# Attention states carried by one scan per head pair, in a kernel of attention and two feed-forward layers

## The chip, the core and the metric

The kernel runs on one core of a Trainium2 chip. The metric is device time in microseconds (us), the median of several executions. One more execution was profiled, and all rows of the trace below come from that one. Engines are named as the profile names them: PE (TensorE, matrix products), DVE (VectorE), ACT (ScalarE), POOL (GpSimd) and SP (SyncE, which issues the DMAs).

## What is computed

Three layers follow each other. The first is a gated linear attention with 4 batches, 8 heads, 768 steps and heads of 48; its output is x with 3072 rows of 384.

```python
def _attn_ref(q, k, v, alpha) -> np.ndarray:
    ...
    for t in range(S):
        state = alpha[:, :, t, :, None] * state + np.einsum('bhd,bhe->bhde', k[:, :, t], v[:, :, t])
        y[:, :, t] = np.einsum('bhd,bhde->bhe', q[:, :, t], state)
```

The second layer is `h = x @ w_in; g = h * np.cos(h); x = g @ w_out` with an inner width of 2048. The third is `h = max(x @ w1, x @ w2, x @ w3); h @ w_out` with an inner width of 768. All data are 32 bits wide.

## The kernel before

**Tiling.** The 3072 tokens form 6 blocks (`u`) of 512. Inside a block the attention runs in 8 chunks of 64 steps and in 4 head pairs (`p`; `k` is the order in which they are taken, the last pair first). A batch has 12 chunks, so a state begins anew at chunk 0 of block 0, chunk 4 of block 1, and so on. The two heads of a pair stand at partitions 0 to 47 and 64 to 111.

**One head pair, `att`.** DVE scans alpha into the products `g` (L370 or L380; in block 0 in two halves) and, from their reciprocals, into a second product written over `al` (L376 or L385). POOL multiplies k by `g` (L372 or L384) and q by `al` (L387). PE transposes k (L392, "T" below), ACT brings that from PSUM as `kt` (L395), and PE makes the scores (L404) and the sums of k times v of each chunk (L409) in two PSUM banks `r[0]` and `r[1]` ("K"); chunk c has its sum in bank c mod 2. The scores are masked into `a`: by DVE straight from PSUM (L420), or in blocks `u < MKP` by ACT (L416) and POOL (L417). The states then go from chunk to chunk: `state(c)` is one DVE instruction on 112 by 48 elements (L428, or the copy L426 where a batch begins), eight per head pair and each dependent on the one before. `d` is each chunk's state times that chunk's whole product, by POOL in two instructions (L440; in block 0 one half comes from ACT, L435). PE multiplies `a` with v (L453) and `d` with q (L459) into one result ("V"), which ACT and DVE (in block 0 ACT and PE, L477) split into a high and a low part.

**The feed-forward layers.** Every product of 128 by 128 by 512 is made of three matmuls on high and low parts. Layer two has 16 units per block, `moe1(i)`: 9 matmuls from x (L501 to L503), a cosine on ACT and DVE (L508 to L513 or L517), a high part on ACT (L514 or L518) and a low part on POOL (L515, for units `GLE1 <= i < GLP1`) or on DVE (L523), then 9 matmuls into `acc` (L528 to L530). A weight block is put together from two words by three DVE instructions (L315 to L317), split by ACT (L320) and POOL (L321); the 32 blocks of layer two are made ready during block 0. Layer three follows (L579 to L581, L587 to L591, L602 to L607).

**Order.** Nothing is reordered by hand. `Program` collects operations with an engine, an estimated duration, the names that they read and write, and a due time; `order` walks through them once and gives each engine its queue, which it then runs strictly in order. The due time of an attention step is `ATT0 + ATTS * k` in units of layer two. Two operations that only read the same name are free of each other in that walk.

Of the kernel before, what the change touches and what calls it, by code (L numbers as in the profile page):

```python
# [49 lines left out]
NQ, NG, NRAW, NIN, NV, NGS = 3, 2, 3, 3, 2, 3  # L50
# [10 lines left out]
GLP1 = 20  # L61
# [182 lines left out]
def tile_kernel(ctx, tc, qka, vv, wt, outT):  # L244
# [32 lines left out]
    inv0 = [ap.tile([PR, LINE], F32, name=f"inv{i}")[:, 0:AL].rearrange("p (c t) -> p c t", c=NC) for i in range(2)]  # L277
# [7 lines left out]
    s_b = [ap.tile([PR, NC, D], F32, name=f"s{p}") for p in range(NP)]  # L285
# [56 lines left out]
    def att(u, k, p, t0):  # L342
        m = u * NP + k
        n, n2 = m % NIN, m % 2
        t, kq_, v, kt, a, s, d, iv = al_b[n], kq_b[n], v_b[m % NV], kt_b[n2], a_b[n2], s_b[p], d_b[n2], inv0[n2]
# [77 lines left out]
        def state(c):  # L423
            o, kvc = s[:, (c + 1) % NC], r[c % 2][0:PR, c // 2 * D:(c // 2 + 1) * D]
            if firsts[c]:
                ve.tensor_copy(o, kvc)  # L426
            else:
                ve.scalar_tensor_tensor(o, s[:, c], g[:, c, 0:1], kvc, ALU.mult, ALU.add)  # L428

        for c in range(NC - 1):  # L430
            op("DVE", 0.2, lambda c=c: state(c), [rk[c % 2], *kgs, (*sk, c)], [(*sk, c + 1)], t0 + 0.25)
            if u < DAC and not firsts[c + 1]:
                for j in range(DAH):
                    w = slice(UP * j, UP * j + D)
                    op("Act", act(D) + 0.21, lambda c=c, j=j, w=w: se.activation(d[w, j, c + 1], s[w, c + 1], AF.Copy, scale=g[w, c + 1, 0:1]),  # L435
                       [*kgs, (*sk, c + 1)], [(dk, j, c + 1)], t0 + 0.25)
        for j in range(2):
            if u >= DAC or j >= DAH:
                w = slice(UP * j, UP * j + D)
                op("Pool", pool(NC * D), lambda j=j, w=w: ge.tensor_tensor(d[w, j], s[w], g[w, :, 0:1].to_broadcast([D, NC, D]), ALU.mult),  # L440
                   [*kgs, *[(*sk, c) for c in range(NC)]], [(dk, j, c) for c in range(NC)], t0 + 0.25)
            elif not firsts[0]:
                w = slice(UP * j, UP * j + D)
                op("Act", act(D) + 0.21, lambda j=j, w=w: se.activation(d[w, j, 0], s[w, 0], AF.Copy, scale=g[w, 0, 0:1]), [*kgs, (*sk, 0)], [(dk, j, 0)], t0 + 0.25)
# [166 lines left out]
    def build():  # L611
# [20 lines left out]
        def setup_rest():  # L632
# [132 lines left out]
```

## Time and profile before

| | |
|---|---|
| median of 3 runs | 818.61 us (815.3 to 819.21) |
| profiled execution | 816.9 us, of which the span in the trace is 815.2 us |
| busy in the span | PE 791.5 us (97%), DVE 476.4 (58%), ACT 360.9 (44%), POOL 192.8 (24%) |
| chain that ended last | PE 84%, DVE 6%, POOL 4%, issue 2%, DMA 2%, ACT 2% |

Busy is the time in which an engine runs at least one instruction; a matmul's end is modelled, so a busy PE may still run below its peak. The time outside the span, 1.7 us, is start and end of the execution. [...]

### The profile page before, as it was taken

The page shows a single profiled execution, that of the slowest core. Times are in us where ns is not written, and L with a number is a line of the kernel's source. Part 1 is how long each engine was busy: PE and PEld are TensorE (multiplying, and loading weights), DVE is VectorE, ACT ScalarE, POOL GpSimd, SP SyncE. Part 2 cuts the span into 40 slices and gives each one's busy share as a digit, 9 for nine tenths or more (in the row PEclk, how much of TensorE's full clock was granted, in tenths as well). Part 3 has the DMA queues.
Part 4 walks back from the last instruction along what each step waited for, and adds up shares of the span by engine and source line. Part 5 has one row for each costly group of instructions (what it writes and reads, how often), then busy time and mean ns, then how long its engine had stood idle before and what let it go on. Part 6 is the DMA issues. An engine that isn't in the chain of part 4 may idle for free.

```text
span 815.2 us, 15114 instructions
## 1 busy us (share of the span) xinstructions
PE 791.5 (97%) x6168; PEld 646.0 (79%) x6168; DVE 476.4 (58%) x924; ACT 360.9 (44%) x667; POOL 192.8 (24%) x191
## 2 busy tenths in 40 slices
PE   7679999999999999999999999999999999999998
PEld 6567778888878878888888788888888888888886
DVE  7988999765786587667679955452232222322221
ACT  4575655555645565555577746531121121112121
POOL 7777876530231023101123200110000000000000
PEclk8789999999999999999999999999999999999999
DMA  9745564430242033103135600412020020200001
GB/s 273 214 132 174 182 209 141 130 93 5 88 147 54 2 115 108 43 1 108 34 107 161 221 23 1 156 58 86 26 83 27 14 91 26 78 27 13 14 27 39
DMA packets 26661, 71.86 MB, mean 88 GB/s; under 512 B 3488, under 2 KB 3488, under 8 KB 26592
## 3 DMA queue, kind: packets, MB, share of 16 engines
q1 hardware_dynamic: 26592, 70.90, 26.9%
q8 instruction: 48, 0.79, 0.4%
q14 instruction: 21, 0.17, 0.1%
HBM read 54.37 MB, written 14.16 MB: 84 GB/s over the span
## 4 chain that ended last, share of the span: by engine, by line
PE 84%; DVE 6%; POOL 4%; issue 2%; DMA 2%; ACT 2%; SPq 0%; POOLq 0%; DVEq 0%; ACTq 0%
PE ps L580 9%; PE ps L579 9%; PE ps L581 9%; PE acc L528 7%; PE ps L501 7%; PE acc L530 7%; PE acc L529 7%; PE ps L503 7%; PE ps L502 7%; PE ps L603 3%; PE ps L602 3%; PE ps L604 3%; PE ps L459 2%; PE ps L404 1%; PE ps L453 1%
## 5 line engine op out<-in xcount | busy, mean ns | idle before, releaser
L501 PE MATMUL ps<-xt,wih 128*128 128x512 f32 x288 | 116.3, 404 | 3.7 <-ACT kt L395 2.2
L528 PE MATMUL acc<-gh,woh 128*128 128x512 f32 x288 | 116.5, 405 | 0.7 <-DVE yy L538 0.5
L530 PE MATMUL acc<-gl,woh 128*128 128x512 f32 x288 | 112.8, 392 | 0.5 <-DVE gl L523 0.4
L502 PE MATMUL ps<-xt,wih 128*128 128x512 f32 x288 | 113.2, 393 | 0.0
L503 PE MATMUL ps<-xt,wil 128*128 128x512 f32 x288 | 113.0, 392 | 0.0
L529 PE MATMUL acc<-gh,wol 128*128 128x512 f32 x288 | 112.4, 390 | 0.0
L517 DVE SCALAR_TENSOR_TENSOR ps<-q,ps 128x512 f32<-128x512 f32 x76 | 52.7, 694 | 56.9 <-ACT q L511 56.7
L589 DVE TENSOR_TENSOR ps<-t,ps 128x512 f32<-128x512 f32 x36 | 25.0, 696 | 103.6 <-PE ps L581 103.5
L510 ACT ACTIVATE q<-q 128x512 f32<-128x512 f32 x96 | 60.5, 631 | 52.3 <-DVE q L509 52.0
L508 ACT ACTIVATE q<-ps 128x512 int32<-128x512 f32 x96 | 57.1, 595 | 57.0 <-PE ps L503 54.6
L509 DVE SCALAR_TENSOR_TENSOR q<-q,ps 128x512 f32<-128x512 int32 x96 | 65.7, 685 | 21.1 <-ACT q L508 20.8
L590 ACT ACTIVATE h<-ps 128x512 fp32r<-128x512 f32 x36 | 21.5, 598 | 112.1 <-DVE ps L589 112.0
L523 DVE TENSOR_TENSOR gl<-ps,gh 128x512 fp32r<-128x512 f32 x76 | 52.1, 686 | 26.7 <-PE ps L503 15.9
L501 PEld LDWEIGHTS ps<-xt,wih 128*128 128x128 f32 x288 | 54.7, 190 | 16.4 <-ACT kt L395 3.2
L440 POOL TENSOR_TENSOR d<-s,g 48x384 f32<-48x384 f32 x44 | 37.0, 842 | 125.5 <-DVE s L428 123.7
L587 DVE TENSOR_TENSOR t<-t,ps 128x512 f32<-128x512 f32 x36 | 24.8, 688 | 71.2 <-PE ps L581 70.4
L528 PEld LDWEIGHTS acc<-gh,woh 128*128 128x128 f32 x288 | 54.0, 188 | 14.9 <-DVE yy L538 2.3
L518 ACT ACTIVATE gh<-ps 128x512 fp32r<-128x512 f32 x76 | 45.4, 598 | 44.0 <-DVE ps L517 41.5
L530 PEld LDWEIGHTS acc<-gl,woh 128*128 128x128 f32 x288 | 54.1, 188 | 13.5 <-DVE gl L523 1.4
L503 PEld LDWEIGHTS ps<-xt,wil 128*128 128x128 f32 x288 | 54.7, 190 | 11.8
L502 PEld LDWEIGHTS ps<-xt,wih 128*128 128x128 f32 x288 | 54.9, 190 | 10.4
L529 PEld LDWEIGHTS acc<-gh,wol 128*128 128x128 f32 x288 | 54.1, 188 | 9.9
(122 smaller groups left out, 1579.4 us busy)
## 6 DMA issues: line engine op xcount, KB each, us to landing
raw<-in_wt SPq DMA_DIRECT2D x56, 384.0 KB, 3.3
kq<-in_qka SPq DMA_DIRECT2D x23, 448.0 KB, 4.2
x1d<-yy SPq DMA_DIRECT2D x18, 512.0 KB, 2.6
xt<-x1d SPq DMA_DIRECT2D x18, 512.0 KB, 4.4
v<-in_vv SPq DMA_DIRECT2D x22, 256.0 KB, 3.2
al<-in_qka SPq DMA_DIRECT2D x24, 228.4 KB, 2.7
outT<-y SPq DMA_DIRECT2D x18, 256.0 KB, 2.0
xt<-yy SPq DMA_DIRECT2D x36, 64.0 KB, 2.6
```

The lines of the kernel that those rows point to most:

```text
L501: pe.matmul(ps, wi["h"][:, f, cc], xt[:, cc, 0], start=(cc == 0), stop=False)
L502: pe.matmul(ps, wi["h"][:, f, cc], xt[:, cc, 1], start=False, stop=False)
L503: pe.matmul(ps, wi["l"][:, f, cc], xt[:, cc, 0], start=False, stop=(cc == NR - 1))
L508: op("Act", act(HB, True), lambda: se.activation(q.bitcast(I32), ps, AF.Copy, scale=INV2PI), [hk], [qk], m)
L509: op("DVE", dve(HB), lambda: ve.scalar_tensor_tensor(q, q.bitcast(I32), -TWOPI, ps, ALU.mult, ALU.add), [hk], [qk], m)
L510: op("Act", act(HB), lambda: se.activation(q, q, AF.Sin, scale=0.5), (), [qk], m)
L528: pe.matmul(acc[c], oh, gh, start=(f == 0), stop=False)
L529: pe.matmul(acc[c], ol, gh, start=False, stop=False)
L530: pe.matmul(acc[c], oh, gl, start=False, stop=(f == NF1 - 1))
L579: pe.matmul(ps, w2t["h"][m][:, f, cc], xt[:, cc, 0], start=(cc == 0), stop=False)
L580: pe.matmul(ps, w2t["h"][m][:, f, cc], xt[:, cc, 1], start=False, stop=False)
L581: pe.matmul(ps, w2t["l"][m][:, f, cc], xt[:, cc, 0], start=False, stop=(cc == NR - 1))
```

## The change

The eight state instructions of a head pair become one DVE scan. The state tile is now laid out as 48 columns of ten places: place 0 holds the state that comes in, places 1 to 8 the sums of k times v of the eight chunks, which ACT copies there from both PSUM banks, and place 9 a zero. A second tile `gx` holds the product of each chunk (0 where a batch begins), then 1 and 0. The scan adds a place of the state tile to what it carries and multiplies by the place of `gx`, so that each chunk's `d` comes out of it directly. ACT first moves place 8 of the block before to place 0. `d` is then copied out of the columns: by ACT and POOL one half each, in block 0 both by ACT (`DC0`). The spread of `g` into `gx` is written to go to ACT in blocks 0 and 1 (`GXA`) and to POOL otherwise; the function `spread` compares `e` when it is called, and at that time `e` holds the last letter given in the loop on `j`, "A" or "P", so that the instruction is a POOL copy in every block. In the walk it counts as ACT's for blocks 0 and 1.

Beside that, the masks of block 0 go to DVE (`MKP` 0), units 20 to 27 have their low part on POOL (`GLP1` 28), there are two `g` tiles and one tile of reciprocals in place of three and two, and the due times change (`W1E`, `MOE_EARLY`, `ATT0`, `ATTS`), as does the estimate of a matmul. `SELU` is 0, so `rest` is never issued, but `setup_sel` is.

```diff
-NQ, NG, NRAW, NIN, NV, NGS = 3, 2, 3, 3, 2, 3
+NQ, NG, NRAW, NIN, NV, NGS = 3, 2, 3, 3, 2, 2
...
-GLP1 = 20
+GLP1 = 28
...
-MKP = 1
-
-DAC = 1
-DAH = 1
-
-
-W1E = 10
-MOE_EARLY = 4
+MKP = 0
+
+GXA = (0, 1)
+DCA = ()
+DC0 = "AA"
+
+SELU = 0
+
+
+W1E = 14
+MOE_EARLY = 6
...
-ATT0 = -3.0
-ATTS = 2.5
+ATT0 = -2
+ATTS = 3
...
 def mm(n, m):
-    return (n + 0.375 * m) / 2400.0
+    return (n + 0.25 * m) / 2400.0
...
-    s_b = [ap.tile([PR, NC, D], F32, name=f"s{p}") for p in range(NP)]
+
+    s_b = [ap.tile([PR, D, NC + 2], F32, name=f"s{p}") for p in range(NP)]
+    x_b = [ap.tile([PR, D, NC + 2], F32, name=f"gx{i}") for i in range(1)]
...
-        for c in range(NC - 1):
-            op("DVE", 0.2, lambda c=c: state(c), [rk[c % 2], *kgs, (*sk, c)], [(*sk, c + 1)], t0 + 0.25)
...
+        gx, xk = x_b[0], ("gx", 0)
+
+        def spread(e):
+            gc = g.rearrange("p c t -> p t c")[:, 0:1].to_broadcast([PR, D, NC])
+            if e == "Act":
+                se.activation(gx[:, :, 0:NC], gc, AF.Copy)
             else:
-                ve.scalar_tensor_tensor(o, s[:, c], g[:, c, 0:1], kvc, ALU.mult, ALU.add)
+                ge.tensor_copy(gx[:, :, 0:NC], gc)
+            for c in range(NC):
+                if firsts[c]:
+                    if e == "Act":
+                        se.activation(gx[:, :, c:c + 1], gc[:, :, c:c + 1], AF.Copy, scale=0.0)
+                    else:
+                        ge.memset(gx[:, :, c:c + 1], 0.0)
+
+        e = "Act" if u in GXA else "Pool"
+        op(e, (act(NC * D) if e == "Act" else pool(NC * D)) + 0.25 * any(firsts), lambda: spread(e), kgs, [xk], t0 - 0.5)
+        if u:
+            op("Act", 0.25, lambda: se.activation(s[:, :, 0:1], s[:, :, NC:NC + 1], AF.Copy), (), [sk], t0 - 0.5)
+        for h in range(2):
+            op("Act", act(AO, True) + 0.05, lambda h=h: se.activation(
+                s[:, :, 1 + h:NC + 1:2], r[h][0:PR, 0:AO].rearrange("p (i e) -> p e i", e=D), AF.Copy), [rk[h], *([sk] if h else [])], [(sk, h) if h else sk], t0 + 0.22)
+        op("DVE", 0.07 + 0.00208 * D * (NC + 2), lambda: ve.tensor_tensor_scan(
+            s.rearrange("p e c -> p (e c)"), s.rearrange("p e c -> p (e c)"), gx.rearrange("p e c -> p (e c)"), 0.0, ALU.add, ALU.mult),
+           [xk, (sk, 1)], [sk], t0 + 0.25, port=True)
         for j in range(2):
...
+            w = slice(UP * j, UP * j + D)
+            e = (DC0 if u == 0 else "AA" if u in DCA else "AP")[j]
+            x = s[w, :, 0:NC].rearrange("p e c -> p c e")
+            if e == "A":
+                op("Act", act(NC * D), lambda j=j, w=w, x=x: se.activation(d[w, j], x, AF.Copy), [sk], [(dk, j)], t0 + 0.25)
...
+            else:
+                op("Pool", pool(NC * D), lambda j=j, w=w, x=x: ge.tensor_copy(d[w, j], x), [sk], [(dk, j)], t0 + 0.25)
...
-            for t in (*s_b, *d_b):
+            for t in (*s_b, *d_b, *x_b):
                 ge.memset(t, 0.0)
```

How the queues change is shown at two places. The first is POOL at the start of the program, in block 0, here before; `kq` and `yy` are tiles of k and q of the four head pairs, `a` the scores, `wil` and `wol` low parts of weights.

```order
L638 MEMSET d_127 112x768
L372 TENSOR_TENSOR kq_110<-kq_110,g_113 112x512
L387 TENSOR_TENSOR kq_110<-kq_110,al_107 112x512
L372 TENSOR_TENSOR kq_111<-kq_111,g_114 112x512
L387 TENSOR_TENSOR kq_111<-kq_111,al_108 112x512
L417 TENSOR_TENSOR a_120<-a_120,tri 128x256 x2
L372 TENSOR_TENSOR kq_112<-kq_112,g_115 112x512
L440 TENSOR_TENSOR d_126<-s_125,g_113 48x384
L387 TENSOR_TENSOR kq_112<-kq_112,al_109 112x512
L417 TENSOR_TENSOR a_121<-a_121,tri 128x256 x2
L440 TENSOR_TENSOR d_127<-s_122,g_114 48x384
```

The same place of POOL in the changed kernel:

```order
L681 MEMSET gx_124 112x480
L683 MEMSET gx_124 112x48
L442 COPY gx_124<-g_112 112x48x8
L448 MEMSET gx_124 112x48
L383 TENSOR_TENSOR kq_109<-kq_109,g_112 112x512
L398 TENSOR_TENSOR kq_109<-kq_109,al_106 112x512
L383 TENSOR_TENSOR kq_110<-kq_110,g_113 112x512
L398 TENSOR_TENSOR kq_110<-kq_110,al_107 112x512
L383 TENSOR_TENSOR kq_111<-kq_111,g_112 112x512
L442 COPY gx_124<-g_113 112x48x8
L448 MEMSET gx_124 112x48
L398 TENSOR_TENSOR kq_111<-kq_111,al_108 112x512
```

Masks and `d` products are gone from POOL, a spread (L442) now stands ahead of the first product of k, and a second one between the two products of the third head pair.

The second place is the last head pair of block 3, between K and V, first on DVE before (`a` the scores, `s` the state, `q` a tile of layer two's cosine; five more steps of the state follow these rows).

```order
L420 TENSOR_TENSOR a_121<-ps_98,tri 128x256
L420 TENSOR_TENSOR a_121<-ps_102,tri 128x256
L426 COPY s_124<-ps_98 112x48
L428 SCALAR_TENSOR_TENSOR s_124<-s_124,g_113,ps_102 112x48
L428 SCALAR_TENSOR_TENSOR s_124<-s_124,g_113,ps_98 112x48
L509 SCALAR_TENSOR_TENSOR q_84<-q_84,ps_101 128x512
```

On DVE in the changed kernel, with what each instruction waits for (the scan, L457, is printed under the name of its instruction form):

```order
L542 SCALAR_TENSOR_TENSOR q_83<-q_83,ps_99 128x512 [waits Activation_49]
L431 TENSOR_TENSOR a_119<-ps_102,tri 128x256 [waits Activation_49]
L431 TENSOR_TENSOR a_119<-ps_100,tri 128x256 [waits PE_49]
L457 SCALAR_TENSOR_TENSOR s_122<-s_122,gx_124 112x480 [waits Activation_49,Pool_49]
L550 SCALAR_TENSOR_TENSOR ps_99<-q_83,ps_99 128x512 [waits Activation_49]
```

On ACT in the changed kernel at the same place, also with waits (L455 are the copies out of the PSUM banks ps_102 and ps_100, L465 is ACT's half of `d`):

```order
L541 ACTIVATE q_83<-ps_99 128x512 [waits PE_49]
L455 ACTIVATE s_122<-ps_102 112x48x4 [waits PE_49]
L543 ACTIVATE q_83<-q_83 128x512 [waits DVE_49]
L455 ACTIVATE s_122<-ps_100 112x48x4 [waits DVE_49]
L544 ACTIVATE q_83<-q_83 128x512 [waits Activation_49]
L465 ACTIVATE d_126<-s_122 48x384 [waits DVE_49]
```

Where DVE ran masks and states by itself, DVE's first mask now waits for ACT's copy out of the same bank, ACT's second copy waits for DVE, and the scan waits for ACT.

## Rows read from the trace of the kernel before

**Rows 1.** Busy time by stage; columns: PE, PEld (weight load), DVE, ACT, POOL, clock, DMA.

```profile
0.00:20.00 20.00, 15.28 (x298) 13.91 (x298) 15.64 (x43) 9.12 (x26) 15.57 (x27) 0.83 0.94 273
20.00:40.00 20.00, 14.01 (x264) 11.11 (x263) 17.90 (x42) 11.64 (x35) 15.44 (x15) 0.75 0.72 216
40.00:60.00 20.00, 15.26 (x168) 11.95 (x169) 17.35 (x37) 13.28 (x26) 15.53 (x14) 0.83 0.40 128
60.00:120.00 60.00, 56.51 (x583) 44.33 (x583) 57.14 (x126) 36.92 (x73) 48.83 (x42) 1.00 0.60 186
120.00:800.00 680.00, 678.95 (x4814) 555.54 (x4814) 367.69 (x679) 287.50 (x506) 97.42 (x95) 1.00 0.21 70
```

**Rows 2.** Waits of PE over the span: us in total, times, longest.

```profile
PE ps L392 <- DVE raw L317: 3.0, 1, 3.0
...
PE acc L528 <- DVE yy L538: 0.5, 1, 0.5
```

**Rows 3.** Waits of DVE in the first 120 us: us in total, times, longest.

```profile
DVE ps L315 <- DMA raw<-in_wt: 2.2, 3, 1.4
DVE s L426 <- ACT a L416: 2.0, 2, 1.0
DVE s L428 <- ACT a L416: 1.4, 3, 0.7
```

**Rows 4.** Groups of instructions by shape over the span: busy us, mean ns, idle before.

```profile
L509 DVE SCALAR_TENSOR_TENSOR q<-q,ps 128x512 f32<-128x512 int32 x96 | 65.7, 685 | 21.1 <-ACT q L508 20.8
...
L428 DVE SCALAR_TENSOR_TENSOR s<-s,g,ps 112x48 f32<-112x48 f32 x176 | 45.5, 259 | 4.8 <-ACT a L416 1.4 <-POOL d L440 0.3
...
L440 POOL TENSOR_TENSOR d<-s,g 48x384 f32<-48x384 f32 x44 | 37.0, 842 | 125.5 <-DVE s L428 123.7
L316 DVE SCALAR_TENSOR_TENSOR ps<-raw,ps 128x384 uint32<-128x384 uint32 x56 | 31.2, 556 | 0.8
...
L385 DVE TENSOR_TENSOR_SCAN al<-al,inv 112x520 f32<-112x520 f32 x20 | 27.0, 1350 | 0.3
...
L420 DVE TENSOR_TENSOR a<-ps,tri 128x256 f32<-128x256 f32 x40 | 15.4, 417 | 3.0 <-PE ps L409 3.0
...
L474 ACT ACTIVATE xt<-ps 128x256 fp32r<-128x256 f32 x30 | 10.3, 377 | 7.3 <-PE ps L459 7.2
...
L320 ACT ACTIVATE wih<-raw 128x384 fp32r<-128x384 f32 x16 | 8.9, 559 | 12.5 <-DVE raw L317 11.8 <-DMA v<-in_vv 0.8
...
L417 POOL TENSOR_TENSOR a<-a,tri 128x256 f32<-128x256 f32 x8 | 5.8, 730 | 4.8 <-ACT a L416 4.7
```

**Rows 5.** PE in order of time, first 62 us: start, length in us.

```profile
17.93 1.13 PE L404 MATMUL ps<-kq 48*64 48x64 f32 x32
...
32.04 0.47 PE L501 MATMUL ps<-xt,wih 128*128 128x512 f32 x1 [1.28 <-DMA xt<-yy]
...
59.88 0.50 PE L528 MATMUL acc<-gh,woh 128*128 128x512 f32 x1
```

**Rows 6.** DVE in order of time, first 62 us.

```profile
48.95 0.69 DVE L509 SCALAR_TENSOR_TENSOR q<-q,ps 128x512 f32<-128x512 int32 x1 [0.30 <-ACT q L508]
```

**Rows 7.** All engines in order of time, 37 to 39 us.

```profile
37.43 1.83 DVE L385 TENSOR_TENSOR_SCAN al<-al,inv 112x520 f32<-112x520 f32 x1
...
38.13 2.10 POOL L387 TENSOR_TENSOR kq<-kq,al 112x512 f32<-112x512 f32 x1
```

**Rows 8.** All engines in order of time, one head pair at 305 us.

```profile
305.74 0.69 PE L404 MATMUL ps<-kq 48*64 48x64 f32 x32
...
306.81 0.50 PE L528 MATMUL acc<-gh,woh 128*128 128x512 f32 x1
...
310.19 1.76 POOL L440 TENSOR_TENSOR d<-s,g 48x384 f32<-48x384 f32 x2 [1.53 <-DVE s L428]
...
313.15 0.69 PE L453 MATMUL ps<-a,v 64*64 64x64 f32 x32
...
314.69 0.50 PE L528 MATMUL acc<-gh,woh 128*128 128x512 f32 x1
```

More of the change, by code (lines that the diff above doesn't have):

```diff
@@ L147, in order @@
         start = [0.0] * n
+        gap = [0.0] * n
         dma_free = 0.0
@@ L173, in order @@
             if e == "PE":
+                gap[i] = t - free[e]
                 if t - free[e] > IDLE:
@@ L205, in order @@
         self.start = start
+        self.gap = gap
+        self.opens = opens
         return sorted(range(n), key=lambda i: (start[i], i)), chosen
@@ L270, in tile_kernel @@
     gl_b = [mp.tile([P, HB], F32R, name=f"gl{i}") for i in range(NG)]
+    sel = gl_b[1][:, 0:(NP - 1) * P].rearrange("p (k n) -> p k n", k=NP - 1)
     yy_b = [mp.tile([P, 2, HB], F32R, name=f"yy{i}") for i in range(2)]
@@ L276, in tile_kernel @@
     one0 = ap.tile([PR, LINE], F32, name="one0")[:, 0:AL].rearrange("p (c t) -> p c t", c=NC)
-    inv0 = [ap.tile([PR, LINE], F32, name=f"inv{i}")[:, 0:AL].rearrange("p (c t) -> p c t", c=NC) for i in range(2)]
+    inv0 = [ap.tile([PR, LINE], F32, name=f"inv{i}")[:, 0:AL].rearrange("p (c t) -> p c t", c=NC) for i in range(1)]
     tri = ap.tile([P, 1, C], F32, name="tri")
@@ L437, in att @@
-        for j in range(2):
[L438 to L444, printed above, removed]
@@ L459, in values @@
                         pe.matmul(y[h][UP * j:UP * j + D, c // 2 * C:(c // 2 + 1) * C], d[:, j, c], qv3[:, c], start=False, stop=False, skip_group_check=True)
-        op("PE", 3 * SWITCH + N2 * mm4(C) + NC * mm4(C), values, [vk, ("a", n2, 0), ("a", n2, 1), *[(dk, j, c) for j in range(2) for c in range(NC)], kq], [*yks, ("done", n2)], t0 + 0.3)
+        moved = u < SELU and p < NP - 1
+        op("PE", 3 * SWITCH + N2 * mm4(C) + NC * mm4(C), values, [vk, ("a", n2, 0), ("a", n2, 1), (dk, 0), (dk, 1), kq], [*yks, ("done", n2)], t0 + 0.3)
         xa = []
@@ L470, in att, with rest @@
             xa = [("xtA", xn)]
+        if moved:
+            def rest():
+                for h in range(2):
+                    for x in range(2):
+                        pe.matmul(y[h][:, 0:HB // 2], sel[:, p], yy_b[0][:, x, HB // 2 * h:HB // 2 * (h + 1)], start=False, stop=(x == 1), skip_group_check=True)
+            op("PE", 0.5, rest, ["sel", ("gl", 1), *[("yy0", x, h) for x in "hl" for h in range(2)]], yks, t0 + 0.3)
         for h in range(2):
@@ L482, in att @@
                     o()[:, 1, cs], y[h][:, 0:HB // 2], o().bitcast(F32)[:, 0, cs], ALU.subtract), [yks[h], *[(*k, h) for k in hk]], [(*k, h) for k in lk], t0 + 0.5)
-        if p < NP - 1:
+        if p < NP - 1 and not moved:
             for i in range(2):
@@ L627, in build, with setup_sel @@
         op("DVE", 0.8, setup, (), [("acc", 2)], due=-99)
-        op("DVE", 1.5, setup_pads, (), ["one0", ("iv", 0), ("iv", 1)], due=-98)
+        op("DVE", 1.5, setup_pads, (), ["one0", ("iv", 0)], due=-98)
         op("Pool", 1.0, lambda: make_identity(nc, ident), (), ["ident"], due=-99)
         op("Act", act(P), lambda: se.activation(minus, ident, AF.Copy, scale=-1.0), ["ident"], ["minus"], due=-98)
+        def setup_sel():
+            for p in range(NP - 1):
+                se.activation(sel[:, p], ident, AF.Copy, scale=0.0)
+                for i in range(2):
+                    row = 16 * (2 * p + i)
+                    src = UP * (row // D) + row % D
+                    se.activation(sel[:, p, UP * i + D:UP * (i + 1)], ident[:, src:src + 16], AF.Copy)
+        op("Act", 2.4, setup_sel, ["ident"], ["sel", ("gl", 1)], due=-97)
         def setup_rest():
```

22 lines of the change are left out of this document (8 added, 14 removed).

## The prediction

> **What bounds the kernel now.** I read the stages first. From 120 to 800 us PE is busy for 678.95 of 680 us, so nothing can be gained there except by less PE work, and the change has the same matmuls as before. [...] The waits of PE tell the same: the longest, 3.0 us, is a transpose behind a weight block on DVE, and of those after 120 us the longest is 0.5 us [rows 2]. So DVE paces the start, because it must put together 32 weight blocks while the attention runs, and PE paces the rest. Some of DVE's own waits there come from what the change touches: 2.0 + 1.4 us in which a state step waits until ACT has read the same PSUM bank for the mask [rows 3].
>
> **DVE per head pair.** Removed are eight state steps of 259 ns, 2.07 us at most, and less where they are interleaved with other work, since their shown lengths then overlap the neighbours'. Added is a scan of 480 places; by the 520-place scan of 1350 ns it takes 1.25 us. From block 1 on that saves up to 0.8 us. In block 0 two masks of 417 ns come to DVE as well, so nothing is saved [rows 4].
>
> **ACT and POOL per head pair.** ACT gains two copies of 192 elements (under 0.38 us each, the 256-wide copy), a carry copy, bounded the same way, and one `d` copy of 384, 0.56 us by the weight's copy of that size: about 1.5 us, 30 us over blocks 1 to 5. ACT is busy for 36.92 of 60 us in the crowded stage, so this is hidden as long as no one waits for a particular copy. POOL loses one product of 842 ns and gains a spread of 384 elements. No row shows a copy with such strides on POOL: by the mask (730 ns for 256 elements) it would be 1.1 us, as one input instead of two perhaps 0.42; I take 0.84, the row of the same size, so POOL is even. In block 0 it loses eight masks and four products, 8 × 0.73 + 4 × 0.84 = 9.2 us, and gains four spreads, 3.4 [rows 4]. That GXA's spreads run on POOL and not on ACT is included. The extra set-up for `sel` stands on ACT before its first copy and costs nothing; the longer memsets and the first spread put the first product of k some 1.5 us later (0.84 for the spread, the rest an estimate).
>
> **The start, at two points.** The third head pair's K (17.93 us before) now stands behind the second pair's V in PE's queue, which waits for scan and copies: by DVE's queue that scan can't end before some 18 us, two `d` copies of 0.56 us and other ACT work put V at 20.9, and V takes 1.54 us or, at the lower clock, up to 3, so K comes at some 23. Its mask holds up DVE by about 2 us, against the 3.4 us of waits on ACT that go. The first unit of layer two, at 32.04, stays within 1 us [rows 5]. Then the queues win. Ahead of the first L509, at 48.95 us [rows 6], DVE had 39 state steps, 24 weight instructions, 6 long scans and 2 masks; now it has 4 short scans, 22, 5 and 10. With steps of 0.2 to 0.26 us that is -7.8 to -10.1 + 5.0 + 8 × 0.42 - 2 × 0.56 - 1.35 = -1.9 to -4.2; I take -3, and -1 for the waits: 45. The first L528, 10.9 us behind it, comes at 56 instead of 59.88. PE has by then done one K more and one V and nine-matmul third less, net 1.15 us: worth 2.8 us.
>
> The later point is the product of the 16th unit, the last that needs new weights. DVE's queue ahead of it has 72 steps, 102 weight instructions and 10 masks before, now 10 scans, 100 and 20, one long scan fewer, one L509 and two mask-sized instructions more: 0 to -3 us, and I take 0, the steps being mostly interleaved. But PE has then done a K (306.81 - 305.74 = 1.07), a V (314.69 - 313.15 = 1.54) and a group of three big matmuls (0.68) more, 3.3 us; (313.15 - 306.81 - 0.2) / 9 gives the 0.68 [rows 8]. With 1 us of waits less it is worth 4.3. From here on nothing that the start has won can be lost but by new waits of PE. I take **4.3 us**, bounds 2.8 and, if DVE's 3 us come on top, 7.3.
>
> **The new chain between K and V.** Before, at 305 us, nine groups of three matmuls stand between K and V (6.3 us), and POOL is done with `d` 1.2 us before V starts [rows 8]; PE never waited. In the new PE queue ten of the sixteen head pairs of blocks 2 to 5 have six groups, 4.3 us, the others seven or more. What must fit is ACT's copy 0.38, the two masks 0.83, ACT's second copy 0.38, the scan 1.25, POOL's `d` 0.84: 3.7 us, as the queues' waits put them one behind the other. That leaves 0.6 us for six hand-overs and for whatever is at work on ACT (0.6), DVE (0.7) or POOL when the chain arrives. Behind a late V all of PE waits. I take 0.05 us on each of sixteen, **0.8 us**; bounds 0 and 13.
>
> [...]
>
> The sum: 816.9 for the profiled execution - 4.3 + 0.8 = 813.4, that is 3.5 us less; on the median of 818.61 this is **815.0**. A measurement can tell about 0.5% from no change, 4.1 us: under 814.5 is faster, over 822.7 slower.
>
> **Rivals.**
>
> *V waits.* The chain does not fit. For it speaks that the spare time is smaller than one foreign instruction on any of its engines, and that ACT and DVE hand over four times; against it that 305 us shows 1.2 us spare in a chain of nine dependent instructions. At 0.8 us on each of fourteen head pairs it costs 11 us instead of 0.8: 825. It decides from 0.5 us per pair on, where it has eaten the start's gain and 0.5% beyond. Chance 0.20. PE's L453 or L459 would show as the largest waits after 120 us.
>
> *Scan against POOL.* At 37 us a scan on DVE took 1.83 us and a product on POOL beside it 2.10, against a mean of 1.35 for such scans [rows 7]. The state steps that go read one tensor from SBUF and one from PSUM; the new scan reads both from SBUF. If each of the nine new scans of the crowded start loses 0.5 us so, 4.5 us go: 819.5, no change. Against it: the planner keeps `port` operations apart, but not the spreads of blocks 0 and 1, which it books on ACT. Chance 0.16. [...]
>
> *More of the start.* DVE's steps count fully and V never waits: 816.9 - 7.3, or 9 with the clock up earlier. The median would be 809 to 811.5. For it speaks that POOL, 80% busy there, is relieved by 6 us, and that 2.2 us of DVE's waits were for weight words whose buffers POOL must free [rows 3]. Chance 0.23.
>
> The forecast itself, 812 to 818.5, has 0.41, of which 0.16 lies under 814.5. So faster is 0.16 + 0.23 = 0.39, slower 0.20 + 0.02, the same 0.39. The range, **808 to 824**, takes in all but the far halves of the first and third rival.
>
> **What would show it.** Right: the first L528's counterpart at 54 to 57 us; PE's idle time in the first 120 us down from 18.9 to about 15; the new scan at 1.2 to 1.3 us; PE at 99.8% from 120 to 800 us again. Wrong: waits of V after 120 us above 4 us together; the spread or `d` copy on POOL over 1.2 us; K of the third pair later than 24 us and the first unit later than 34; the scan's mean over 1.6.

## The result and the profile after

The changed kernel takes 824.11 us (median of 4 runs, 822.54 to 825.19), the kernel before 818.09 beside it: a ratio of 1.009, 95% interval 1.007 to 1.0109. In a later series it was 823.61 against 817.63, 1.0068 (1.0049 to 1.0087). So it is slower by some 6 us; 815.0 was forecast, with a range up to 824. The profiled execution took 823.97 us, its span 822.3, against 816.9 and 815.2.

Busy time by stage of the changed kernel, columns as in [rows 1]; the clock is the one granted to TensorE, as a share of its full speed:

```profile
0.00:20.00 20.00, 13.91 (x254) 12.34 (x258) 16.63 (x33) 10.15 (x26) 15.75 (x29) 0.89 0.94 286
20.00:40.00 20.00, 15.50 (x290) 12.68 (x282) 17.31 (x28) 10.79 (x25) 12.20 (x11) 0.60 0.67 185
40.00:60.00 20.00, 14.42 (x190) 11.22 (x192) 18.09 (x29) 14.37 (x29) 11.98 (x11) 0.83 0.39 115
60.00:120.00 60.00, 55.43 (x648) 43.16 (x639) 56.47 (x98) 39.29 (x81) 46.92 (x44) 1.00 0.57 166
120.00:800.00 680.00, 677.05 (x4737) 553.46 (x4736) 358.04 (x567) 311.78 (x572) 120.68 (x115) 1.00 0.23 73
```

In the first 120 us PE is now idle for 6.09 + 4.50 + 5.58 + 4.57 = 20.7 us, where it was 18.9 [rows 1]. From 120 to 800 us it is idle for 2.95 us instead of 1.05. The longest waits of PE in the changed kernel (total, times, longest), which answer to [rows 2]:

```profile
PE acc L483 <- ACT d L465: 6.2, 6, 1.8
PE ps L534 <- DVE q L546: 3.6, 1, 3.6
...
PE acc L561 <- DVE yy L571: 2.6, 3, 2.0
```

The first is V of block 0, behind ACT's copies of `d`. The third lies far behind the start, with its longest wait at 472 us. Groups of the changed kernel, as in [rows 4]:

```profile
L457 DVE TENSOR_TENSOR_SCAN s<-s,gx 112x480 f32<-112x480 f32 x24 | 30.5, 1271 | 4.8 <-ACT s L455 4.7
L391 DVE TENSOR_TENSOR_SCAN g<-al,one 112x520 f32<-112x520 f32 x20 | 30.2, 1514 | 1.1 <-POOL gx L442 1.1
...
L465 ACT ACTIVATE d<-s 48x384 f32<-48x384 f32 x28 | 25.8, 923 | 14.8 <-DVE s L457 13.3 <-DVE acc L386 1.4
L442 POOL COPY gx<-g 112x384 f32<-112x384 f32 x24 | 21.6, 901 | 6.8 <-DVE s L457 4.8 <-DVE g L391 1.2
```

The new scan is as long as forecast on the mean, POOL's copies nearly so, ACT's copy of `d` is not. The milestones of PE and DVE, as in [rows 5, 6]:

```profile
22.30 1.13 PE L415 MATMUL ps<-kq 48*64 48x64 f32 x32
...
34.18 0.63 PE L534 MATMUL ps<-xt,wih 128*128 128x512 f32 x1
...
60.26 0.50 PE L561 MATMUL acc<-gh,woh 128*128 128x512 f32 x1
```

```profile
49.93 0.67 DVE L542 SCALAR_TENSOR_TENSOR q<-q,ps 128x512 f32<-128x512 int32 x1
```

K of the third head pair came at 22.30 (forecast 23), but the first L542 at 49.93 instead of 45, and the first L561 at 60.26 instead of 56.

What stood ahead of the first L542 on DVE is the row on which the forecast broke. Busy time up to that point, before (first fence) and after (second):

```profile
0.00:48.90 48.90, 36.49 (x646) 30.91 (x647) 41.88 (x104) 24.66 (x69) 38.54 (x48) 0.79 0.79 234
```

```profile
0.00:49.90 49.90, 37.36 (x649) 31.43 (x650) 43.62 (x72) 26.54 (x63) 35.11 (x47) 0.79 0.75 221
```

DVE has 72 instructions instead of 104, and is busy for 43.62 us instead of 41.88. The long scans up to there, before and after:

```profile
L385 DVE TENSOR_TENSOR_SCAN al<-al,inv 112x520 f32<-112x520 f32 x3 | 4.8, 1599 | 0.0
...
L380 DVE TENSOR_TENSOR_SCAN g<-al,one 112x520 f32<-112x520 f32 x3 | 3.8, 1284 | 0.0
```

```profile
L391 DVE TENSOR_TENSOR_SCAN g<-al,one 112x520 f32<-112x520 f32 x3 | 6.9, 2331 | 0.0
L457 DVE TENSOR_TENSOR_SCAN s<-s,gx 112x480 f32<-112x480 f32 x4 | 6.3, 1588 | 0.3 <-ACT s L455 0.3
...
L396 DVE TENSOR_TENSOR_SCAN al<-al,inv 112x520 f32<-112x520 f32 x2 | 3.3, 1654 | 0.0
```

Undisturbed, later in the same trace, the lengths of 520 and 480 take 1.23 and 1.15 us. Nine scans thus cost 16.5 us where they should cost 10.8, 5.7 more; before, six cost 8.6 where 7.4 would do, 1.2 more. Two of the nine, each with the POOL product that runs when it begins, in order of time:

```profile
36.87 1.20 POOL L395 TENSOR_TENSOR kq<-kq,g 112x512 f32<-112x512 f32 x1
36.97 2.11 DVE L457 TENSOR_TENSOR_SCAN s<-s,gx 112x480 f32<-112x480 f32 x1
...
45.63 1.20 POOL L398 TENSOR_TENSOR kq<-kq,al 112x512 f32<-112x512 f32 x1
45.88 3.01 DVE L391 TENSOR_TENSOR_SCAN g<-al,one 112x520 f32<-112x520 f32 x1
```

Beside the second one, POOL goes on with a low part of a weight (L332) from 46.77 to 47.80 us.

After 120 us nothing of the new chain is ever late. The head pair at 303 us, in order of time:

```profile
303.30 0.69 PE L415 MATMUL ps<-kq 48*64 48x64 f32 x32
...
307.11 1.15 DVE L457 TENSOR_TENSOR_SCAN s<-s,gx 112x480 f32<-112x480 f32 x1
308.39 0.93 ACT L465 ACTIVATE d<-s 48x384 f32<-48x384 f32 x1
308.39 0.91 POOL L469 COPY d<-s 48x384 f32<-48x384 f32 x1 [7.32 <-DVE s L457]
...
310.03 0.69 PE L477 MATMUL ps<-a,v 64*64 64x64 f32 x32
```

POOL is done with `d` at 309.30, 0.7 us before V starts, and PE's only waits after 120 us are those for L571 and one of 0.2 us. The place of the long one, all engines in order of time:

```profile
470.54 0.60 ACT L541 ACTIVATE q<-ps 128x512 int32<-128x512 f32 x1 [1.03 <-PE ps L536]
...
471.04 0.59 ACT L570 ACTIVATE yy<-acc 128x512 fp32r<-128x512 f32 x1
...
471.80 0.68 DVE L571 SCALAR_TENSOR_TENSOR yy<-acc,yy 128x512 fp32r<-128x512 f32 x1
...
472.54 0.59 PE L561 MATMUL acc<-gh,woh 128*128 128x512 f32 x1 [2.03 <-DVE yy L571]
...
473.78 0.63 PE L561 MATMUL acc<-gh,woh 128*128 128x512 f32 x1
...
474.20 0.63 PE L562 MATMUL acc<-gh,wol 128*128 128x512 f32 x1
```

It is the end of layer two for block 4. ACT takes the third result out of `acc` (L570) only behind an L541 that itself waits for PE; the next block's first product needs that bank. And behind the wait the matmuls come 0.42 us apart instead of the 0.23 of 466.25 and 466.48 us: the granted clock of 472 to 476 us is 0.60 on the mean, and 0.50 from 473 to 476 us; at 466 us it is 1.00. Before, the same place cost waits of 0.5 and 0.4 us, at a clock of 1.00.

### The profile page after: what moved, and what is told of

It reads as the page before. It is cut to its first block, busy times and chain, and to the rows that moved or that the text cites. A ratio compares the mean times of both kernels' runs of the same rounds, so it can differ in the third digit from the quotient of the medians.

```text
span 822.3 us, 15035 instructions
## 1 busy us (share of the span) xinstructions
PE 794.8 (97%) x6168; PEld 647.9 (79%) x6168; DVE 470.0 (57%) x755; ACT 390.0 (47%) x736; POOL 207.5 (25%) x209
## 4 chain that ended last, share of the span: by engine, by line
PE 75%; DVE 8%; issue 6%; POOL 6%; ACT 3%; DMA 2%; POOLq 0%; DVEq 0%; SPq 0%; ACTq 0%
PE ps L612 9%; PE ps L613 9%; PE ps L614 9%; PE acc L561 6%; PE acc L563 6%; PE acc L562 6%; PE ps L534 6%; PE ps L536 5%; PE ps L535 5%; PE ps L635 3%; PE ps L636 3%; PE ps L637 3%; DMA raw<-in_wt 1%; PE ps L415 1%; PE ps L483 1%
## 5 line engine op out<-in xcount | busy, mean ns | idle before, releaser
L561 PE MATMUL acc<-gh,woh 128*128 128x512 f32 x288 | 116.9, 406 | 2.6 <-DVE yy L571 2.6
L542 DVE SCALAR_TENSOR_TENSOR q<-q,ps 128x512 f32<-128x512 int32 x96 | 65.4, 682 | 29.4 <-ACT q L541 29.1
L543 ACT ACTIVATE q<-q 128x512 f32<-128x512 f32 x96 | 60.6, 631 | 45.1 <-DVE q L542 44.7
L541 ACT ACTIVATE q<-ps 128x512 int32<-128x512 f32 x96 | 56.9, 593 | 43.7 <-PE ps L536 42.1
L550 DVE SCALAR_TENSOR_TENSOR ps<-q,ps 128x512 f32<-128x512 f32 x68 | 46.9, 689 | 39.4 <-ACT q L544 39.2
L534 PEld LDWEIGHTS ps<-xt,wih 128*128 128x128 f32 x288 | 54.6, 190 | 16.5 <-DVE q L546 3.8
L561 PEld LDWEIGHTS acc<-gh,woh 128*128 128x128 f32 x288 | 54.1, 188 | 16.1 <-DVE yy L571 3.8
L556 DVE TENSOR_TENSOR gl<-ps,gh 128x512 fp32r<-128x512 f32 x68 | 46.5, 687 | 32.3 <-ACT gh L551 23.7
L544 ACT ACTIVATE q<-q 128x512 f32<-128x512 f32 x96 | 60.0, 625 | 1.6
L551 ACT ACTIVATE gh<-ps 128x512 fp32r<-128x512 f32 x68 | 40.4, 595 | 31.2 <-DVE ps L550 28.8
```

The costliest lines, as they stand in the source:

```text
L534: pe.matmul(ps, wi["h"][:, f, cc], xt[:, cc, 0], start=(cc == 0), stop=False)
L542: op("DVE", dve(HB), lambda: ve.scalar_tensor_tensor(q, q.bitcast(I32), -TWOPI, ps, ALU.mult, ALU.add), [hk], [qk], m)
L543: op("Act", act(HB), lambda: se.activation(q, q, AF.Sin, scale=0.5), (), [qk], m)
L544: op("Act", act(HB), lambda: se.activation(q, q, AF.Square), (), [qk], m)
L561: pe.matmul(acc[c], oh, gh, start=(f == 0), stop=False)
```

## The experiments

One trace tells the start to a microsecond or two only: in a second profile of the same kernel the first L542 came at 50.55 instead of 49.93, and twelve runs of one kernel (spreads on ACT, below) lay between 817.34 and 821.75 us. Where less matters, the medians decide. All runs keep the change but for what each edit shows; the yardstick is 824.11, and 823.61 for the last series.

### What the instructions cost side by side

Two lists of prices. In the first, instructions of one group ran into the next, so that it can be read only in part; the second keeps the groups apart.

> No part of the computation: eight repeats each of the disputed instructions, alone and beside each other, on tiles of the kernel's shapes; the output is zeros. Theory A (a scan with two inputs in SBUF and a POOL product shut each other out): scan alone 1.14 us and product alone 1.18; side by side both groups take about 2.3 us per pair; the state step with one input in PSUM stays at 0.26 us beside the product, and so does a scan with one input in PSUM at 1.15. Rival: side by side both stay within 10% of their times alone, and the long scans in the kernel have another cause. ACT's copy reading every tenth place 0.92 us, contiguous 0.52, writing 48 places apart between these two; POOL's copy 0.85 to 0.9 either way.

> No part of the computation, the output is zeros: the same groups of eight as in the first price list, but issued in the order written, with all three engines brought together between groups, so that each pairing stands by itself. From the mixed rows of the first list: scan alone 1.15 us, product alone 1.26, side by side 1.8 to 2.0 each; state step 0.25 alone and 0.26 beside the product; scan with one input in PSUM 1.16 beside the product; POOL's copy 0.85 when it reads every tenth place and 0.50 contiguous; scan beside that strided copy 1.6 to 2.0; ACT's copy 0.88, 0.52 contiguous, 0.86 when it writes 48 places apart, and unchanged beside a scan. Rival: alone in its pairing, the scan stays within 10% of 1.15 us beside POOL.

The groups of the second list; L301 is the scan alone, L304 POOL's product alone, L307 and L308 the two side by side, L312 the state step alone, L316 and L317 beside the product, L320 and L321 a scan with its second input in PSUM beside the product:

```profile
L307 DVE TENSOR_TENSOR_SCAN s<-s,gx 112x480 f32<-112x480 f32 x8 | 15.5, 1942 | 0.2
L308 POOL TENSOR_TENSOR kq<-kq,al 112x512 f32<-112x512 f32 x8 | 15.2, 1900 | 0.5
...
L321 POOL TENSOR_TENSOR kq<-kq,al 112x512 f32<-112x512 f32 x8 | 10.1, 1263 | 0.6
L304 POOL TENSOR_TENSOR kq<-kq,al 112x512 f32<-112x512 f32 x8 | 10.1, 1262 | 0.6
L320 DVE TENSOR_TENSOR_SCAN r<-s,r 112x480 f32<-112x480 f32 x8 | 9.3, 1160 | 0.2
L301 DVE TENSOR_TENSOR_SCAN s<-s,gx 112x480 f32<-112x480 f32 x8 | 9.2, 1156 | 0.2
...
L312 DVE SCALAR_TENSOR_TENSOR st<-st,g,r 112x48 f32<-112x48 f32 x32 | 7.8, 263 | 0.8
L316 DVE SCALAR_TENSOR_TENSOR st<-st,g,r 112x48 f32<-112x48 f32 x32 | 7.8, 263 | 0.8
...
L334 ACT ACTIVATE d<-s 48x384 f32<-48x384 f32 x8 | 7.0, 873 | 0.2
L324 POOL COPY d<-s 48x384 f32<-48x384 f32 x8 | 6.8, 849 | 0.5
...
L340 ACT ACTIVATE d<-s 48x384 f32<-48x384 f32 x8 | 6.7, 842 | 0.2
...
L337 ACT ACTIVATE d<-s 48x384 f32<-48x384 f32 x8 | 4.2, 519 | 0.2
L327 POOL COPY d<-s 48x384 f32<-48x384 f32 x8 | 4.0, 502 | 0.5
```

Side by side the scan takes 1942 ns instead of 1156, the product 1900 instead of 1262. The state step that was removed doesn't notice POOL, 263 ns both ways, and a scan with one input in PSUM doesn't either, 1160 ns beside a product of 1263. The lower rows are the copies of 384: every tenth place read (L334 on ACT, L324 on POOL), written 48 places apart (L340), contiguous (L337, L327). The prediction had no row of a copy with such steps on POOL: reading every tenth place takes 849 ns against 502, 69% more. The rival of "within 10%" is out. A scan beside POOL's copy that reads every tenth place took 1512 ns on the mean, a little under the 1.6 to 2.0 us expected, and the copy 1536 instead of 849: such copies collide with scans as well.

### A scan of the kernel that cannot collide

```diff
-            ..., gx.rearrange("p e c -> p (e c)"), 0.0, ALU.add, ALU.mult),
+            ..., gx.rearrange("p e c -> p (e c)") if u else acc[2][0:PR, 0:D * (NC + 2)], 0.0, ALU.add, ALU.mult),
```

> The changed kernel with one operand moved: block 0's four state scans take their factors from a PSUM bank (acc 2) instead of gx in SBUF, so their values are not the states; lengths and queues are the same. If scans are stretched because both inputs and POOL's inputs lie in SBUF, these four fall from 1588 ns on average to 1150 to 1200, DVE has 1.7 us less ahead of the first L542, and the time falls by 1 to 3 us, to 821 to 823. If the stretch has another cause, they stay at 1.6 us and the time at 824.

Measured: 823.68 us, 1.0074 (1.0054 to 1.0094). The four scans fell to 1140 ns, and one beside a POOL product shows that neither is stretched any more, in order of time:

```profile
39.68 1.20 POOL L395 TENSOR_TENSOR kq<-kq,g 112x512 f32<-112x512 f32 x1
39.72 1.15 DVE L457 TENSOR_TENSOR_SCAN s<-s,acc 112x480 f32<-112x480 f32 x1
```

So in the kernel, too, the stretch went once the scans' second input lay in PSUM, but the 1.8 us that DVE got back in block 0 did not move the median, which was expected to fall by 1 to 3 us, and the first L542 came later, at 51.73. The interval would leave room for a gain of about 1 us; what these four collisions cost is not measured by this run.

### What the scans' time on DVE is worth

```diff
-            s.rearrange("p e c -> p (e c)"), s.rearrange("p e c -> p (e c)"), gx.rearrange("p e c -> p (e c)"), 0.0, ALU.add, ALU.mult),
+            *(x.rearrange("p e c -> p (e c)")[:, 0:(D if u < 2 else D * (NC + 2))] for x in (s, s, gx)), 0.0, ALU.add, ALU.mult),
```

The second run has `u < 1` in place of `u < 2`.

> The changed kernel with the state scans of blocks 0 and 1 over 48 places instead of 480 (so the states of these blocks are not computed); all else and the queues are the same. It takes 1.0 us and what they are stretched by from each of eight scans on DVE. If DVE paces the start, as the prediction had it, 5 us of DVE work ahead of the first L542 go, that comes at about 45 us, and the time falls by 4 or more, to 820 or less. If the start is paced by the chain over ACT (copies of the state, then of d), the first L542 gains 2 us at most and the time stays at 822 or more.

> The changed kernel with the state scans of block 0 alone over 48 places instead of 480 (so the states of that block are not computed); block 1's scans are whole again. Theory 1 (DVE's time counts wherever it is saved before 120 us): DVE loses 4.4 of the 8.3 us that the run with both blocks saved, and the time falls by 3, to 821. Theory 2 (in block 0 the chain over ACT and PE sets the pace, as the run with the PSUM operand suggests, and DVE only from block 1 on): 1 us at most, 823 to 824.

Measured: 818.29 us, 1.0019 (1.0004 to 1.0033), with both blocks short; 820.73, 1.0033 (1.0014 to 1.0053), with block 0 alone. The first L542 came at 48.27 and 49.49, not at 45, but the lead grew: by 122 us the same PE instructions stood 5.5 us earlier than in the changed kernel with both blocks short, 1.1 us with block 0. In block 0 the four scans fell from 6.3 to 1.9 us, in block 1 from 5.7 to 1.8: 4.4 and 3.9 us of DVE. Against 823.61 that brought 2.9 us, and 5.3 for both together (4.0 by the ratios): about 0.65 us for each that DVE is spared, the number of theory 1. But in both runs 1.6 us of PE's lead appear only between 470 and 477 us, since the clock did not fall there (next section). Without that share 1.3 us are left for block 0 and 2.4 to 3.7 for both, 0.3 to 0.45 us for each. So theory 1 met its number for block 0 partly by luck: in the start itself that block gave little more than the 1 us of theory 2, as the run with the PSUM operand also has it. With the scans almost free the time is that of before; the spreads on POOL and the wait of 2.0 us at the end of block 4 were still there, and what free scans would bring without these was not run.

### The spreads back on ACT

```diff
-        op(e, ..., lambda: spread(e), kgs, [xk], t0 - 0.5)
+        op(e, ..., lambda e=e: spread(e), kgs, [xk], t0 - 0.5)
```

> The changed kernel with one edit: the spread's engine is bound where the operation is made, so that in blocks 0 and 1 the eight spreads and their memsets run on ACT, as the planner books them, and no longer on POOL. The queues are the same otherwise, row for row. Theory A (the scans on DVE are stretched by POOL's spreads, which the planner does not see): the long scans fall from 1514 ns towards the 1251 ns of before, the first L542 comes at about 47 us instead of 49.93, and the time falls to about 820. Theory B (ACT's copies of d hold V in block 0): ACT gets eight copies of 0.9 us and eight memsets more, V's waits on ACT in block 0 grow from 6.2 us to 8 or more, and the time is 824 to 826. Theory C (the new constants of the schedule): no change, 824.

Measured: 820.24 us, 1.0027 (1.0012 to 1.0041). The time is what theory A gave; its way there is not. L391 fell only to 1475 ns, L396 from 1426 to 1362, the first L542 stayed at 50.25, and V's waits on ACT went down, to 4.9 us. POOL's busy time in the first 60 us fell from 39.9 to 33.0 us. By 148 us PE stood 1.7 us ahead, and at 477 us 3.2: there the wait was the same, 2.0 us, but the clock stayed up, which is worth 1.6 us between 470 and 477 us. The window of the changed kernel, then of this one:

```profile
472.00:476.00 4.00, 3.46 (x9) 2.69 (x10) 3.86 (x7) 2.86 (x6) 2.05 (x2) 0.60 0.78 273
```

```profile
472.00:476.00 4.00, 4.00 (x19) 3.31 (x18) 3.40 (x7) 1.67 (x4) 1.03 (x1) 1.00 0.85 284
```

### The copies of d

```diff
-                op("Act", act(NC * D), lambda j=j, w=w, x=x: se.activation(d[w, j], x, AF.Copy), [sk], [(dk, j)], t0 + 0.25)
+                op("Act", act(NC * D), lambda j=j, w=w: se.activation(d[w, j].rearrange("p c e -> p (c e)"), s[w].rearrange("p e c -> p (e c)")[:, 0:NC * D], AF.Copy), [sk], [(dk, j)], t0 + 0.25)
```

> The changed kernel with one edit: ACT's d copies read 384 places that stand side by side in the state's tile instead of every tenth, so the values in d are not the states (this part of the computation is changed); sizes, queues and waits are the same. By the weight's copy of the same size such a copy should take 0.56 us instead of 0.92. Theory B (V in block 0 waits for the slow copies): V's waits on ACT fall from 6.2 us to 2 to 3, and the time to 820 or 821. Theories A and C: the waits move elsewhere in the start, whose pace is DVE's, and the time stays at 823.5 to 824.5.

The same values, walked in the other order:

```diff
-            x = s[w, :, 0:NC].rearrange("p e c -> p c e")
+            x = s[w, :, 0:NC]
...
+                op("Act", act(NC * D), lambda j=j, w=w, x=x: se.activation(d[w, j].rearrange("p c e -> p e c"), x, AF.Copy), [sk], [(dk, j)], t0 + 0.25)
```

> The changed kernel with the copies of d, on ACT and on POOL, walked in the other order: they read the state's places as they lie (eight of every ten) and write d 48 places apart. The same values come out, and the queues are the same. If it is the reading of every tenth place that makes ACT's copy 923 ns instead of 523, the copy falls to 0.55 us, V's waits on ACT in block 0 to about 2.3 us, and the time to 821, as with the copy of contiguous places. If steps cost the same on the side that is written, the copy stays at 0.9 us and the time at 824.

And contiguous copies with the spreads on ACT:

> The changed kernel with both earlier edits: blocks 0 and 1 spread on ACT, and ACT's d copies read 384 contiguous places (so the values in d are not the states). If the two losses are separate, the gains of 3.9 and 2.9 us add up and the time is about 817, that of the kernel before. If both only remove the same wait, it stays at 820 to 821.

Measured: contiguous 821.26, 1.0042 (1.0028 to 1.0056), the copy 523 ns, V's waits on ACT 2.3 us. Other order 823.6, 1.0077 (1.0058 to 1.0095), the copy still 898 ns: it moves the steps to the side that is written, and they cost about the same. Both edits 820.85, 1.0044 (1.0026 to 1.0061): no more than either alone, V's waits gone or not. The clock stood at 1.00 behind the wait at 472 us in the first and the third, at 0.63 in the second. So each of these gains holds the 1.6 us that belong to that place and not to the copies or spreads. That is part of why they don't add up: 3.9 + 2.9 - 1.6 would be 5.2 us below 824.11, and 3.3 were measured. The rest of the difference stays open.

### Masks and constants of the schedule

`e3_oldtimes` and `e4_before_newtimes` exchange the six constants, `e10_masks` sets `MKP` to 1, and `e12_scan_alone` does both, so that little more than the scan is left of the change. It also sets `mm2`, the same estimate for layer three, to 0.375, where both kernels have 0.25. The edits together, without `mm2`:

```diff
-GLP1 = 28
+GLP1 = 20
...
-MKP = 0
+MKP = 1
...
-W1E = 14
-MOE_EARLY = 6
+W1E = 10
+MOE_EARLY = 4
...
-ATT0 = -2
-ATTS = 3
+ATT0 = -3.0
+ATTS = 2.5
...
-    return (n + 0.25 * m) / 2400.0
+    return (n + 0.375 * m) / 2400.0
```

> The changed kernel with the six constants of the schedule of the kernel before (GLP1 20, W1E 10, MOE_EARLY 4, ATT0 -3.0, ATTS 2.5, and 0.375 in mm); the scan, the spreads and the copies stay as in the change. Theory C (the constants cost the time: the attention is issued later against the weights, and PE stalls at the end of the first layer-two stage): about 819, with the stall of 2 us at 472 us gone and the PE loss by 150 us some 3 us lower. Theories A and B (the scan and its copies cost it): 823 to 824.5.

> The kernel before, with the six constants of the changed kernel's schedule (GLP1 28, W1E 14, MOE_EARLY 6, ATT0 -2, ATTS 3, 0.25 in mm); the state is still made step by step. Theory C: it loses what the change loses, about 822 to 824. Theories A and B: it stays within 2 us of 818.

> The changed kernel with block 0's masks back on ACT and POOL, as before (MKP 1), planned anew: DVE loses eight masks of 0.417 us and the 2.5 to 2.9 us that they wait for ACT's copies out of the same bank; POOL gains eight products of 0.73 us, ACT eight copies. If DVE's load is what counts, the first L542 comes at 45 to 46 us and the time is 819 to 821. If it is the scans' collisions with POOL, POOL's extra work stretches them further, L542 stays at 49 or later and the time at 823 or more.

> The state by scan, and of the rest of the change as little as possible: masks of block 0 on ACT and POOL and the six constants of the schedule as before, planned anew. If the scans with their copies cost what the change loses, 823 to 826. If the loss lies in the masks and the constants, 817 to 819.

Measured: the change with the old constants 830.48, 1.0156 (1.0131 to 1.0181); the kernel before with the new ones 818.45, 1.0009 (0.9991 to 1.0026); the change with the old masks 826.55, 1.0115 (1.0094 to 1.0136), where L457 is stretched to 1349 ns on the mean and the first L542 comes at 54.33, the outcome expected if collisions count, though a fuller POOL queue alone could give it too; scan alone 824.98, 1.0097 (1.0074 to 1.012). Theory C falls: the constants cost the old kernel nothing and save the new one 6 us. The loss comes with the scan and what all these runs keep with it: its copies and spreads, fewer tiles for `g` and its reciprocals, and the set-up of `sel`. The tiles and the set-up were not tested by themselves.

### The end of block 4

The second result of that block leaves through a buffer that attention no longer uses, so that the third need not wait for the second's DMA; the queues are the same up to about 460 us.

```diff
-                yn = 1
+                yn = 0 if (i, c) == (79, 1) else 1
```

> The changed kernel once more, as a yardstick beside the next three and for a second profile. If the fall of PE's clock behind the stall at 472 us belongs to this order of work, the new profile shows it again (0.6 to 0.8 from 472 to 476 us); if it comes by chance, it will be missing in about half of such profiles. The time: 823.5 to 824.5.

> The changed kernel with one edit: at the end of the fifth block of layer two the middle one of the three results leaves through the buffer yy0, which attention no longer uses, instead of yy1, so that the third needs not wait for its DMA; the orders are the same up to about 460 us. If PE's stall of 2.0 us and the lower clock behind it are a cost of their own, on top of the start, the time falls by 2 to 3.5, to 820.5 to 822. If PE only waits there for what it would wait for a little later (weights of the last layer), it stays at 823.5 or more.

> Both: the spreads of blocks 0 and 1 on ACT, and the end of the fifth block without the wait. If the first edit's 3.9 us were all won in the start, the gains add up: 817 to 818.5. If about 1.6 of them were the clock that did not fall at 472 us, the two share that: 818.5 to 820.5.

Measured: the changed kernel again 823.61, 1.0068 (1.0049 to 1.0087), and its second profile shows the clock at 0.61 from 472 to 476 us; without the wait 820.24, 1.0028 (1.0015 to 1.0041); with the spreads on ACT as well 817.40, 0.9999 (0.9985 to 1.0014). Here the gains add up: 3.4 us for the end of the block, 2.8 us for the spreads, this time with no clock fall in either; of the 3.9 us for the spreads further up, 2.3 are left without the clock's 1.6. In the trace of the run without the wait, the window that showed 0.60:

```profile
472.00:476.00 4.00, 4.00 (x19) 3.31 (x18) 3.57 (x7) 2.95 (x6) 1.10 (x2) 1.00 0.47 142
```

### Letting PE do the steps

On top of both edits, `d` is laid out like the state, so that the copies run along it and PE loads every eighth place.

```diff
-    d_b = [ap.tile([PR, 2, NC, D], F32, name=f"d{i}") for i in range(2)]
+    d_b = [ap.tile([PR, 2, D, NC], F32, name=f"d{i}") for i in range(2)]
...
-            x = s[w, :, 0:NC].rearrange("p e c -> p c e")
+            x = s[w, :, 0:NC]
...
-                        pe.matmul(..., d[:, j, c], qv3[:, c], ...)
+                        pe.matmul(..., d[:, j, :, c], qv3[:, c], ...)
```

> The better version so far (spreads of blocks 0 and 1 on ACT, end of the fifth block without the wait), and d laid out as the state is: the copies run along it, and PE, when it loads d as weights, reads every eighth place. If PE's weight load doesn't mind (123 ns for 112 x 48 before), ACT's copy falls from 0.92 to 0.55 us and POOL's from 0.90 to 0.55, V's waits on ACT in block 0 from 5.7 to about 2.3 us, and the time by 1 to 3 us below 817.4: faster than both kernels. If PE pays for the steps, 20 ns on each of some 700 loads cost up to 14 us, unless they hide behind the matmuls: 817 to 831.

Measured: 826.55 us, 1.012 (1.0101 to 1.014). The copies fell to 523 ns on ACT and 545 on POOL, and PE paid. Groups without the steps, then with them:

```profile
L483 PE MATMUL ps<-kq,d 112*48 112x64 f32 x592 | 20.7, 222 | 0.0
...
L483 PEld LDWEIGHTS ps<-kq,d 112*48 112x48 f32 x592 | 17.7, 123 | 1.3
```

```profile
L483 PE MATMUL ps<-kq,d 112*48 112x64 f32 x592 | 31.6, 258 | 0.0
...
L483 PEld LDWEIGHTS ps<-kq,d 112*48 112x48 f32 x592 | 28.8, 188 | 1.3
```

PE is busy for 31.6 us with them instead of 20.7, which is more than the 9.1 us lost between the two medians. What the steps of ACT's copies cost the start by themselves stays open: at most the 2.4 to 2.9 us by which the contiguous copies were faster than 823.61 and 824.11, and 1.6 of that is the clock.

## Why the prediction was wrong

**What bounds the kernel.** Right: all of the new chain's trouble lies in the first 120 us. Incomplete: the prediction counted on PE at 99.8% from 120 to 800 us and looked at the order around K and V alone. At the end of block 4 the new queues put ACT's third L570 behind an L541, and a wait of 2.03 us with a lower clock behind it followed. Without wait and fall the kernel is 3.4 us faster. The kernel before lost 0.9 us there, so the excess is about 2.5. The place was there to be seen: its predecessor is the second row of [rows 2]. The lower clock at which the forecast for K counts V is in the trace of before: 0.50 from 36.65 us, where V took 2.80 us, against 1.54 at 1.00 from 313.15 us. What a clock that is up earlier would bring, the step from 7.3 to 9 us in "More of the start", no run shows.

**DVE ahead of the first L509: the step that failed.** It said 3 us less work, first L542 at 45. DVE had 1.7 us more (43.62 against 41.88), 4.7 us off, and that is nearly all by which L542 missed its forecast, 4.9 us; DVE's idle time up to there fell from 7.0 to 6.3 us, near the 1 us forecast. The first unit of layer two came 2.1 us later than before, not within 1. The count of instructions was right; the scans were not at 1.25 and 1.35 us each but 1.59 to 2.33, since they stood beside POOL's products of k, q and weights: 5.7 us of stretch against 1.2 before. The prices (1942 against 1156 ns) and the run with the PSUM operand (1140 against 1588) show that the product beside them stretches scans with both inputs in SBUF. What this costs in time is shown only for DVE's time as a whole, 0.3 to 0.45 us for each without the clock's share; by that the 4.5 us more of stretch are worth an estimated 1.4 to 2 us. The one run that took away stretch alone, in block 0, showed no gain.

**The rival "Scan against POOL"** had thus the right cause, with a chance of 0.16. Its size, 4.5 us of DVE, was met by luck: it laid them on nine new scans, and here 1.7 us fell on four new scans and 2.8 on the scans of alpha, which were there before. And it put 4.5 us of time on them, two to three times the 1.4 to 2 that the runs suggest. Its argument against itself, that the planner keeps `port` operations apart, broke: the walk's times are not the chip's, and the colliding ones are mostly booked as `port`, L332, L395 and L398, as in the two pairs shown above.

**POOL "even" in the spread.** The price was right, 0.90 against 0.84 us. The conclusion, that spreads on POOL cost nothing, was 2.8 us off, by the difference of 820.24 and 817.40. Whether by POOL's queue or by collisions with scans was not separated: the long scans of alpha fell only from 1514 to 1475 and from 1426 to 1362 ns.

**ACT's copy of d** was mis-sized, 0.92 us instead of 0.56: the row of a contiguous copy was taken for one that reads every tenth place, though the same question was asked for POOL's. In block 0, with two of them ahead of V, PE waited 6.2 us.

**The chain between K and V** was taken at 0.8 us, its rival at 11. It cost nothing: 0.7 us were to spare at 303 us, and V never waited after 120 us.

**The sum.** Forecast were 3.5 us less (818.61 less 3.5 is 815.1 rather than 815.0, which changes nothing); 6 more were measured. The end of block 4, about 2.5, the spreads, 2.8, and the stretched scans, an estimated 1.4 to 2, make some 7 of the 9.5 us between them, the last two perhaps with some overlap. ACT's copies may hold another 0.8 to 1.3 us, their gain without the clock's share; the rest stays open. That with spreads and stall mended the kernel stands at 0.9999 of before shows where the 6 us lie. That the gain of 3.5 us did not come either is argued from DVE's busy time, whose relief was never there; no run shows the gain with the stretch taken away.

## What to carry to other kernels

Price an instruction by what runs beside it: a VectorE scan with both inputs in SBUF took 1.9 us beside a POOL product instead of 1.15, while the small PSUM-fed steps that it replaced took 263 ns both ways. When a change re-plans the queues, read the new order also at the places where the bounding engine has its few remaining waits, since a wait of 2 us there, with the lower clock of 0.60 behind it, cost 3.4. A gain that vanishes when two edits are joined may belong to a third place that both happen to shift; undo that place first, then add.

## What the hardware showed that was not expected

Steps between 32-bit places cost ACT about the same on reading and writing, 873 and 842 ns against 519 contiguous for 48 by 384; reading with steps took POOL 849 against 502. PE is not exempt: its weight load of 112 by 48 went from 123 to 188 ns with every eighth place.

Behind a PE wait of 2.0 us at 472 us the granted clock fell to about 0.6 in both profiles of the changed kernel, and stayed below 0.8 in those of the run with the other walking order (0.63) and with the PSUM operand (0.79), while in the kernels with the spreads on ACT, with contiguous copies, or with short scans a wait as long left it at 1.00. After waits of 2.1 to 2.5 us it fell in other plans too: to 0.66 with the old masks, to 0.57 with the old constants, to 0.74 with the scan alone, and to 0.66 in the kernel before with the new constants, whose time stayed that of before. What decides whether it falls no run shows.
